# Attention and MLP on one core: a new hand-written order for the first two tiles and three batches

## The chip, the cores and the metric

One NeuronCore of a Trainium2 chip runs the program. The metric is the device time of one execution in microseconds (us). Five engines work from queues of their own, in order, and wait for each other through semaphores: TensorE (PE), VectorE (DVE), ScalarE (ACT), GpSimd (POOL) and SyncE (SP), which here only issues transfers.

## The reference

Attention within a window, eight batches, eight heads, 576 positions, 64 values a head:

```
scores = scale * q @ k^T ; scores = where(0 <= i-j < 128, scores + slope_h * -|i-j|, -1e9)
attn = softmax(scores) ; a = attn @ v
x = a.transpose(0, 2, 1, 3).reshape(4608, 512)
h = x @ w_in                       # 512 -> 2048
g = 0.5 * h * (1 + erf(h / sqrt(2)))
out = g @ w_out                    # 2048 -> 512
```

All arrays are fp32.

## The kernel before

The tokens are cut into nine tiles of 512 (`t` = 0 to 8); a batch of 576 positions fills one tile and a little of the next. A matrix product is made of three fp16 products: each operand is split into a high and a low half, the high half written by ACT, the low half by DVE (`low_part`, L219 or L218), and high by high, high by low and low by high are summed in PSUM. Only batch 0's attention and the second product of tile 0 run in fp32.

Per batch and pair of heads (four pairs, names `_0` to `_3`) the steps are: scores on PE (`sc`, L515), bias added on DVE (`s`, L546; batch 0: on PE, L529), row maxima on DVE, exponentials on ACT (`s<-s,nmax`, L639; batch 0: L590), weights split into `e_main` (high on POOL or ACT, low on DVE), transposed by a transfer (`et<-e_main`, L658; batch 0: by PE and copied by ACT, L618, L626), weighing on PE (`av<-et,vbuf`, L700), and leaving into the tile's slice of `x` (`x<-av`, high L720 on ACT, low on DVE). Before a batch begins, `q`, `k` and `v` are split (`qbuf`, `kbuf`, `vbuf`). The words of the weights are joined and split too (`raw`, `zi`, `wi` for `w_in`; `raw`, `zo`, `wo` for `w_out`; L255 to L277).

Per tile there are sixteen blocks of 128 features: twelve matmuls `h` each (L747), four slices of `x` by three products; a gelu (L764 for tile 0, L770 behind it) on ACT, split by POOL and DVE into `g`; and then four output blocks `o` (L790 in fp32, L793), each copied out by `put` (`ob`, ACT for odd, DVE for even blocks, L804 and L806) and sent off. Each function is a Python generator that issues one or a few instructions between its `yield`s.

Two tables of numbers rule the first part. `ORDER` lists the steps of batches 0, 1, 2 and tiles 0, 1 and the loads that belong to them: each word names a generator (`s1`: scores of pair 1 of batch 0, `S1`, `2S1` the same of batches 1 and 2; `l3`: leaving of pair 3; `H4`, `1H4`: features block 4 of tiles 0 and 1; `g`, `o`, `k`: gelu, output block, put; `i`, `j`, `J`: splitting and joining of weights), and the program goes through the words and advances that generator by one `yield`. The words so set the order in each engine's queue, SP's too. `PSUM_BANKS` gives, in the order in which tiles of PSUM are opened, the bank (0 to 7) that each takes. Tiles 2 to 8 come from a regular loop. A `put` takes one of three rooms `ob`, which the 32-bit gelu results share.

Of the kernel before, what the change touches and what calls it, by code (L numbers as in the profile page):

```python
# [1364 lines left out]
```

## Time and profile before

| | us |
|---|---|
| median of three runs | 885.46 (885.32 to 887.59) |
| profiled execution | 886.68 |
| its span in the trace | 884.8 |
| PE busy | 864.7 (98%) |
| DVE busy | 710.0 (80%) |
| ACT busy | 549.5 (62%) |
| POOL busy | 194.6 (22%) |

The span is what the trace covers from the first to the last instruction; 1.88 us of the execution lie outside of it. PE's matmuls overlap, so its busy time is the time in which at least one runs.

### The profile page before, as it was taken

The numbers are of one execution on the slowest core, as the hardware profiler recorded it, in microseconds if no ns is written. First come the engines' busy times: TensorE is split into PE (matmuls) and PEld (weight loads), VectorE is DVE, ScalarE is ACT, GpSimd is POOL, SyncE is SP. The second block draws the span as 40 slices with busy tenths as digits, with TensorE's granted clock in tenths as the row PEclk, the third lists the DMA queues.
The fourth block names the chain that finished last, engine by engine and source line by source line (L and its number), as shares of the span: only waits on it lengthen the run. The fifth ranks groups of instructions, "written<-read, shape, count | busy, mean of one in ns | idle before, by whom it ended". The sixth has DMA issues, their size and how long they took to land.

```text
span 884.8 us, 18584 instructions
## 1 busy us (share of the span) xinstructions
PE 864.7 (98%) x7428; PEld 478.5 (54%) x7428; DVE 710.0 (80%) x1388; ACT 549.5 (62%) x1149; POOL 194.6 (22%) x412
## 2 busy tenths in 40 slices
PE   5899999999999999999999999999999999999998
PEld 3654454544544445445455545454545454588887
DVE  6999999898858886788678884888477889999871
ACT  7999999787635564554464553567355338744760
POOL 1010010121104521353115521534054310000000
PEclk9899999999999999999999999999999999999999
DMA  9757492545380546225622275234222230001001
GB/s 330 249 160 276 168 216 61 157 138 112 88 253 1 97 78 187 70 62 113 185 73 55 57 159 162 54 54 95 62 56 54 74 71 12 1 13 37 1 1 48
DMA packets 174598, 91.63 MB, mean 104 GB/s; under 512 B 133680, under 2 KB 156336, under 8 KB 174384
## 3 DMA queue, kind: packets, MB, share of 16 engines
q1 hardware_dynamic: 174512, 90.45, 38.3%
q8 instruction: 58, 0.95, 0.5%
q14 instruction: 28, 0.23, 0.1%
HBM read 46.53 MB, written 9.44 MB: 63 GB/s over the span
## 4 chain that ended last, share of the span: by engine, by line
PE 78%; DVE 6%; ACT 2%; DMA 2%; issue 2%; POOL 0%; ACTq 0%; DVEq 0%; POOLq 0%
PE h L747 26%; PE o L793 26%; PE o L790 5%; PE av L700 5%; PE u_out L1082 4%; PE sc L515 3%; PE u L995 2%; PE v L995 2%; DVE g L219 2%; PE z_out L1082 1%; PE x_out L1082 1%; PE y_out L1082 1%; PE v_out L1082 1%; DMA et<-e_main 1%; DVE e_main L219 1%
## 5 line engine op out<-in xcount | busy, mean ns | idle before, releaser
L747 PE MATMUL h<-x,wi 128*128 128x512 f16 x1536 | 339.8, 379 | 2.9 <-ACT g L770 2.0
L747 PEld LDWEIGHTS <-wi 128*128 128x128 f16 x1536 | 148.3, 98 | 184.9 <-issue 9.4
L793 PE MATMUL o<-wo,g 128*128 128x512 f16 x864 | 192.3, 379 | 0.0
L793 PEld LDWEIGHTS <-g 128*128 128x128 f16 x1152 | 110.8, 98 | 132.5
L639 ACT ACTIVATE s<-s,nmax 128x192 f32<-128x192 f32 x252 | 110.9, 441 | 42.0 <-DVE nmax L636 41.9
L219 DVE SCALAR_TENSOR_TENSOR e_main<-s,z,e_main 128x192 f16<-128x192 f32 x252 | 117.6, 509 | 13.5 <-POOL e_main L648 10.4
L771 POOL TENSOR_SCALAR g<-g,sg 128x512 f16<-128x512 f32 x96 | 76.3, 802 | 236.6 <-ACT g L770 229.2
L770 ACT ACTIVATE g<-h,gs 128x512 f32<-128x512 f32 x96 | 63.6, 686 | 86.1 <-PE h L747 56.2
L219 DVE SCALAR_TENSOR_TENSOR g<-g,sg,g 128x512 f16<-128x512 f32 x96 | 80.8, 859 | 31.4 <-POOL g L771 31.4
L648 POOL TENSOR_SCALAR e_main<-s,z 128x192 f16<-128x192 f32 x180 | 89.3, 516 | 66.8 <-ACT s L639 37.9
L546 DVE SCALAR_TENSOR_TENSOR s<-sc,cs,bias_h 128x384 f32<-128x384 f32 x112 | 63.9, 608 | 9.7 <-PE sc L515 9.6
L720 ACT ACTIVATE x<-av,cx 128x128 f16<-128x128 f32 (+6 forms) x52 | 24.6, 481 | 67.2 <-PE av L700 62.8
L793 PE MATMUL o<-wo_first,g 128*128 128x512 f16 x288 | 65.8, 379 | 0.0
L515 PE MATMUL sc<-kbuf,qbuf 64*64 64x192 f16 (+3 forms) x1656 | 48.7, 252 | 10.1 <-DMA kbuf<-kp 5.2
L790 PE MATMUL o<-zo,g 128*128 128x512 f32 x128 | 58.4, 596 | 0.0
L636 DVE TENSOR_REDUCE nmax<-s 128x5 f32<-128x960 f32 (+1 forms) x56 | 56.6, 1044 | 1.0 <-POOL s L552 0.8
L552 POOL MEMSET s<- 64x128 f32 (+1 forms) x112 | 19.3, 172 | 144.8 <-DVE s L546 142.7
L219 DVE SCALAR_TENSOR_TENSOR x<-av,cx,x 128x448 f16<-128x448 f32 (+6 forms) x52 | 24.7, 491 | 29.3 <-ACT x L720 29.2
L639 ACT ACTIVATION_READ_ACCUMULATOR s<-s,nmax 128x1 f32 x252 | 47.1, 187 | 0.0
L700 PEld LDWEIGHTS <-vbuf 128*64 128x64 f16 x1680 | 40.3, 111 | 9.6 <-issue 7.6
L700 PE MATMUL av<-et,vbuf 128*64 128x128 f16 (+1 forms) x1680 | 42.9, 210 | 0.1
L1082 PEld LDWEIGHTS <-g 128*128 128x128 f16 x384 | 37.6, 98 | 4.5
(269 smaller groups left out, 1127.2 us busy)
## 6 DMA issues: line engine op xcount, KB each, us to landing
v<-vp SPq DMA_DIRECT2D x32, 320.0 KB, 5.0
out<-ob SPq DMA_DIRECT2D x34, 256.0 KB, 2.2
raw<-w_in SPq DMA_DIRECT2D x8, 1024.0 KB, 10.5
raw<-w_out SPq DMA_DIRECT2D x8, 1024.0 KB, 5.5
q<-qp SPq DMA_DIRECT2D x7, 1152.0 KB, 6.1
k<-kp SPq DMA_DIRECT2D x7, 1152.0 KB, 7.5
qbuf<-qp SPq DMA_DIRECT2D x4, 288.0 KB, 5.1
kbuf<-kp SPq DMA_DIRECT2D x4, 288.0 KB, 6.7
```

The lines of the kernel that those rows point to most:

```text
L219: return nc.vector.scalar_tensor_tensor(out=dst, in0=src, scalar=scale, in1=high, op0=ALU.mult, op1=ALU.subtract)
L515: done = nc.tensor.matmul(ps[bank][o, n, gap:W], a, m[:, gap:W], start=(i == 0 and (n == 0 or b > 0)), stop=(i == len(terms) - 1 and b > 0 ...
L546: yield nc.vector.scalar_tensor_tensor(out=s[:, bank[0] : bank[0] + k, :], in0=ps[bank][:, 0:k, 0:W], scalar=cs, in1=bias.broadcast_to([P, ...
L639: yield nc.scalar.activation(s[:, i, :], s[:, i, :], AF.Exp, bias=nmax[:, i : i + 1], accum_out=z[:, i : i + 1])
L648: yield nc.gpsimd.tensor_scalar(e[:, i, 0, c], s[:, i], z[:, i : i + 1], 1.0, op0=ALU.mult, op1=ALU.mult)
L700: done = nc.tensor.matmul(av[r, (j - blocks[0]) * QB : (j - blocks[0] + len(js)) * QB], v32s[b][:, hp, kb, r] if b < EXACT else vbuf[:, vi ...
L747: done = nc.tensor.matmul(ph, wi[n][:, a, cc, k * P : (k + 1) * P], x[:, cc, b, :], start=(i == 0), stop=(i == 3 * NCC - 1),)
L770: yield nc.scalar.activation(g32, ph, AF.Gelu, scale=gsc[t, n])
L771: yield nc.gpsimd.tensor_scalar(g[:, r, 0], g32, gsg[t, n], 1.0, op0=ALU.mult, op1=ALU.mult)
L790: done = nc.tensor.matmul(o, g[:, r, c], zo[n][:, n % 2, k * DM : (k + 1) * DM], start=(fc == first), stop=(fc == last))
L793: done = nc.tensor.matmul(o, g[:, r, a, c], wo[n][:, b, k, :], start=(fc == first and i == 0), stop=(fc == last and i == 2),)
L1082: nc.tensor.matmul(ps[name][:, tb], f(d, a)[:, k, tb * P : (tb + 1) * P], w(d, b, k), start=first, stop=True, skip_group_check=True,)
```

## The change

New numbers in `ORDER` and `PSUM_BANKS`. The buffers of a pair (`s`, `nmax`, `z`, `et`) are made when a step first asks for them, no longer by the step of the first part, so that steps may come in another order; for the same reason the join of words looks its target up later and the gelu its `g`. The regular loop is not touched. Two lines of the table, and the code:

```
-z0 z0 z0 b b z1 b z1 z1 z2 b F z2 F s0 m00 m00 s0 m00 x00 x00 x00 x00 s0 x00 n00 n00 s1 m01 z2 x01 x01 m01 z2 x01
+z0 z0 z0 b b s0 s0 s0 m00 m00 m00 z1 z1 z1 x00 x00 m01 x00 x00 x00 z2 m01 x01 b b s1 x01 z2 m10 x01 n00 z2 x10 m10 s1
...
-        raw = raws.pop(n)
+        raw = raws[n]
         lo, hi = raw[:, :, 0], raw[:, :, 1]
-        zi = z.bitcast(I32)
...
+        zi = z().bitcast(I32)
...
-        yield from join_words(n, zi[n])
+        yield from join_words(n, lambda: zi[n])
...
+        def __getattr__(self, name):
+
+            u, hp = self.u, self.hp
+            if name in ("nmax", "z"):
+                made = small([P, NG], f"{name}{u}", 2, tag=name)
+            elif name == "s":
+                made = room([P, NG, W], F32, "s", f"s{u}", 2)
+            elif name == "et":
+                k = 1 if self.b < EXACT else 2
+                made = pool.tile([P, NG * 2 * k, P], F16 if k > 1 else F32, tag=f"et{hp % 2}", name=f"et{u}", bufs=1)
+            else:
+                raise AttributeError(name)
+            setattr(self, name, made)
+            return made
...
-        g = g_of[t, q]
         if t == 0:
-            yield nc.scalar.activation(g[:, r], ph, AF.Gelu, scale=gsc[t, n])
+            yield nc.scalar.activation(g_of[t, q][:, r], ph, AF.Gelu, scale=gsc[t, n])
```

The code lost a few lines above these places, so line numbers differ by one (helpers) to fourteen between the two kernels.

DVE at the leaving of batch 0's pairs, before. `x_410` is `x` of tile 0, `av_3_0` the weighing of pair 3 of batch 0; `zi` and `wi` are words and halves of `w_in`:

```order
L256 TENSOR_SCALAR zi_585,stw_586<-zi_585 128x1024 x2
L266 SCALAR_TENSOR_TENSOR zi_585<-zi_585,raw_363 128x1024
L269 SCALAR_TENSOR_TENSOR zi_585<-raw_363,zi_585 128x1024
L219 SCALAR_TENSOR_TENSOR x_410<-av_2_0_545,scv_450,x_410 128x512
L266 SCALAR_TENSOR_TENSOR zi_585<-zi_585,raw_439 128x1024
L219 SCALAR_TENSOR_TENSOR wi_647<-zi_261,sww,wi_647 128x1024
L185 TENSOR_SCALAR stw_586<-stw_586 128x2
L266 SCALAR_TENSOR_TENSOR zi_261<-zi_261,raw_316 128x1024
L312 TENSOR_TENSOR stw_586<-stw_586 128x1
L219 SCALAR_TENSOR_TENSOR x_410<-av_3_0_650,scv_450,x_410 128x512
```

And after, the same place:

```order
L218 SCALAR_TENSOR_TENSOR x_466<-av_1_0_508,scv_476,x_466 128x512
L255 TENSOR_SCALAR zi_653,stw_654<-zi_653 128x1024
L218 SCALAR_TENSOR_TENSOR x_466<-av_2_0_570,scv_476,x_466 128x512
L255 TENSOR_SCALAR zi_653,stw_654<-zi_653 128x1024
L218 SCALAR_TENSOR_TENSOR x_466<-av_3_0_631,scv_476,x_466 128x512
L218 SCALAR_TENSOR_TENSOR wi_688<-zi_345,sww,wi_688 128x1024
L184 TENSOR_SCALAR stw_654<-stw_654 128x2
L311 TENSOR_TENSOR stw_654<-stw_654 128x1
```

The joins of two words of `zi`, a third join (two of them half done) and one low half of `wi` stood before the slice of pair 3 and stand behind it now.

ACT at the same place, before (`et_3` is the copy of pair 3's transposed weights):

```order
L720 ACTIVATE x_410<-av_2_0_545,scv_450 128x512
L626 COPY et_3_595<-tp_3_5_617 128x512
L626 COPY et_3_595<-tp_3_7_630 128x512
L263 ACTIVATE raw_439<-raw_439 128x1024
L716 COPY tail<-av_3_1_636 128x64
L277 ACTIVATE wi_647<-zi_261,sww 128x1024
L263 ACTIVATE raw_316<-raw_316 128x1024
L720 ACTIVATE x_410<-av_3_0_650,scv_450 128x512
```

And after:

```order
L631 COPY et_3_568<-tp_3_7_615 128x512
L720 ACTIVATE x_466<-av_1_0_508,scv_476 128x512
L254 ACTIVATE zi_653<-raw_478 128x1024
L720 ACTIVATE x_466<-av_2_0_570,scv_476 128x512
L254 ACTIVATE zi_653<-raw_490 128x1024
L720 ACTIVATE x_466<-av_3_0_631,scv_476 128x512
L276 ACTIVATE wi_688<-zi_345,sww 128x1024
L261 ACTIVATE raw_436<-raw_436 128x1024
L261 ACTIVATE raw_490<-raw_490 128x1024
```

The joins and the split have gone behind the slice of pair 3.

ACT at the end of tile 1, before (`ob_1`, `ob_3` are copies of output blocks 1 and 3 of tile 1, `g_2_0` the first gelu of tile 2):

```order
L720 ACTIVATE x_2902<-av_3_3_3078,cx_3_2893 128x192
L422 ACTIVATE vbuf<-v_3_2122,scv_2384 128x2560
L720 ACTIVATE x_1721<-av_3_2_3103,cx_2_2328 128x384
L804 ACTIVATE ob_1_3157<-o_1_2621,so_2719 128x512
L804 ACTIVATE ob_3_3176<-o_3_2576,so_2719 128x512
L770 ACT_TABLE_LOAD
L770 ACTIVATE g_2_0_3208<-h_0_3194,gs_0_3188 128x512
```

And after:

```order
L720 ACTIVATE x_1719<-av_3_2_3086,cx_2_2977 128x384
L804 ACTIVATE ob_1_3128<-o_1_2543,so_1394 128x512
L421 ACTIVATE vbuf<-v_3_2287,scv_2472 128x2560
L720 ACTIVATE x_2921<-av_3_3_3131,cx_3_2914 128x192
L720 ACTIVATE x_2921<-av_1_3_2753,cx_3_2914 128x192
L769 ACT_TABLE_LOAD
L769 ACTIVATE g_2_0_3208<-h_0_3194,gs_0_3188 128x512
```

`ob_3` has moved ten rows forward and `ob_1` stands ahead of the split of `v`; the last copy of the tile is now one of DVE's.

## Rows read from the trace of the kernel before

**Rows 1.** The page: busy time of the engines over the span, with share and instructions.

```profile
PE 864.7 (98%) x7428; PEld 478.5 (54%) x7428; DVE 710.0 (80%) x1388; ACT 549.5 (62%) x1149; POOL 194.6 (22%) x412
```

**Rows 2.** Busy time in five stretches of the span: start and end, length, then busy us (and instructions) of each engine, the granted clock of PE, the busy share of the DMA engines and GB/s.

```profile
0.00:53.00 53.00, 40.95 (x435) 28.36 (x436) 43.42 (x90) 47.82 (x123) 6.05 (x19) 0.94 0.73 242
53.00:165.00 112.00, 111.63 (x791) 53.36 (x791) 105.98 (x217) 105.17 (x188) 6.90 (x21) 1.00 0.67 194
165.00:255.00 90.00, 88.06 (x814) 44.37 (x810) 79.04 (x158) 66.08 (x150) 15.06 (x32) 1.00 0.51 132
255.00:323.00 68.00, 65.98 (x614) 32.58 (x611) 52.64 (x113) 32.68 (x81) 27.67 (x55) 1.00 0.33 79
323.00:884.00 561.00, 558.12 (x4793) 319.85 (x4788) 428.94 (x814) 297.76 (x609) 138.88 (x285) 1.00 0.29 71
```

**Rows 3.** What PE waited for over the whole span: engine, line and output that waited, what released it; us in total, times, longest.

```profile
PE sc L515 <- ACT s L590: 2.7, 4, 1.7
PE tp L618 <- ACT s L590: 2.1, 3, 1.2
...
PE h L747 <- ACT g L770: 2.0, 2, 1.3
```

**Rows 4.** The same columns as rows 2, for 20 to 56 us in steps of 6; the last row is the sum.

```profile
20.00:26.00 6.00, 4.47 (x47) 3.01 (x48) 6.00 (x13) 6.00 (x23) 0.00 (x0) 0.70 1.11 329
26.00:32.00 6.00, 5.90 (x62) 4.63 (x63) 5.96 (x19) 5.49 (x15) 0.35 (x1) 0.73 1.03 375
...
sum 36.00, PE 32.36 PEld 22.68 DVE 35.12 ACT 35.49 POOL 3.48; mean PE 5.39 PEld 3.78 DVE 5.85 ACT 5.92 POOL 0.58
```

**Rows 5.** Timeline of PE, start us, us, engine, line, operation, tiles, count, and idle time before it with what ended it.

```profile
52.58 9.67 PE L747 MATMUL h<-x,wi 128*128 128x512 f16 x44
```

**Rows 6.** Timeline of ACT and of DVE around the fourth slice of `x` of tile 0.

```profile
51.40 1.44 ACT L277 ACTIVATE wi<-zi,sww 128x1024 f16<-128x1024 f32 x1
52.45 1.43 ACT L263 ACTIVATE raw<-raw 128x1024 int32<-128x1024 uint32 x1
53.49 0.95 ACT L720 ACTIVATE x<-av,scv 128x512 f16<-128x512 f32 x1
...
54.14 1.22 DVE L266 SCALAR_TENSOR_TENSOR zi<-zi,raw 128x1024 int32<-128x1024 int32 x1
55.35 0.74 DVE L219 SCALAR_TENSOR_TENSOR x<-av,scv,x 128x512 f16<-128x512 f32 x1
```

**Rows 7.** The same columns as rows 2, from the start to two points: the end of the fourth slice of `x` on DVE, and the end of the last low half of the fourth pair of batch 1.

```profile
0.00:56.09 56.09, 44.04 (x450) 29.77 (x451) 46.52 (x96) 50.91 (x126) 6.05 (x19) 0.94 0.73 240
0.00:158.88 158.88, 146.46 (x1157) 78.50 (x1158) 145.48 (x299) 146.87 (x306) 12.95 (x40) 0.98 0.68 208
```

**Rows 8.** Timeline of PE at the start of tile 2.

```profile
255.11 10.52 PE L747 MATMUL h<-x,wi 128*128 128x512 f16 x48
266.33 2.75 PE L747 MATMUL h<-x,wi 128*128 128x512 f16 x12 [0.69 <-ACT g L770]
...
291.03 1.24 PE L747 MATMUL h<-x,wi 128*128 128x512 f16 x5 [1.30 <-ACT g L770]
```

**Rows 9.** Timeline of ACT there.

```profile
249.75 2.43 ACT L422 ACTIVATE vbuf<-v,scv 128x2560 f16<-128x2560 f32 x1
...
262.02 0.69 ACT L804 ACTIVATE ob<-o,so 128x512 f32<-128x512 f32 x1 [8.79 <-DMA out<-ob]
264.30 1.28 ACT L770 ACT_TABLE_LOAD   x1 [1.59 <-DMA out<-ob]
265.59 1.84 ACT L770 ACTIVATE g<-h,gs 128x512 f32<-128x512 f32 x3
...
273.02 0.69 ACT L770 ACTIVATE g<-h,gs 128x512 f32<-128x512 f32 x1 [2.87 <-PE h L747]
273.73 1.28 ACT L639 ACT_TABLE_LOAD   x1
```

**Rows 10.** Timeline of DVE there.

```profile
267.10 4.46 DVE L219 SCALAR_TENSOR_TENSOR g<-g,sg,g 128x512 f16<-128x512 f32 x4 [4.14 <-POOL g L771]
...
289.17 1.03 DVE L219 SCALAR_TENSOR_TENSOR g<-g,sg,g 128x512 f16<-128x512 f32 x1
```

**Rows 11.** Timeline of PE, the three waits of scores in tile 1.

```profile
172.68 0.83 PE L515 MATMUL sc<-kbuf,qbuf 64*64 64x192 f16 x29 [0.61 <-ACT g L770]
...
208.07 0.88 PE L515 MATMUL sc<-kbuf,qbuf 64*64 64x192 f16 x30 [0.85 <-ACT g L770]
...
222.39 0.69 PE L515 MATMUL sc<-kbuf,qbuf 64*64 64x192 f16 x24 [0.38 <-DVE s L546]
```

**Rows 12.** Timeline of DVE and of PE at the fourth pair of batch 1, and the time from issue to landing of the transposing transfers `et<-e_main` of 120 to 170 us.

```profile
150.89 0.42 DVE L219 SCALAR_TENSOR_TENSOR e_main<-s,z,e_main 128x192 f16<-128x192 f32 x1 [0.21 <-ACT e_main L646]
...
158.47 0.41 DVE L219 SCALAR_TENSOR_TENSOR e_main<-s,z,e_main 128x192 f16<-128x192 f32 x1
...
163.91 1.60 PE L700 MATMUL av<-et,vbuf 128*64 128x128 f16 x66
...
DMA to landing us min/median/max: 3.8/4.2/5.0
```

**Rows 13.** Timeline of DVE and of PE at the first scores of batch 1.

```profile
90.09 2.61 DVE L219 SCALAR_TENSOR_TENSOR kbuf<-k,scq,kbuf 128x2304 f16<-128x2304 f32 x1
...
93.54 1.44 PE L515 MATMUL sc<-kbuf,qbuf 64*64 64x192 f16 x48
```

More of the change, by code (lines that the diff above doesn't have):

```diff
@@ new lines @@
+e0 e0 t0 t1 e1 x30 x30 z W0 t2 s3 j1 e0 n21 a2 x30 L0 m30 x30 z s3 x30 j1 z j0 m31 n30 j1 p0 n30 t0 t1 n30 p0 p0 z t2
+F a3 t1 t1 e0 w0 v0 e1 t3 n21 v0 F p0 e2 e1 e1 W1 F L1 e2 t2 a3 e2 p0 n21 x31 x31 m31 x31 v0 v0 x31 w1 t3 i1 t2 t2 e2
+cl n31 n31 n31 v0 e2 l0 p1 t3 i1 p1 p1 i0 W2 t3 p1 e3 w2 l0 H3 F i0 d d d H2 p1 p0 d L2 e3 j2 j2 e3 e3 H1 t3 H0 j2 W3
+e3 w3 l1 l1 F H1 a4 H2 a4 l2 l2 a5 f a5 H3 lv lv lv H1 H0 H0 p2 l3 l3 H0 i2 i2 j3 H2 H4 lv p2 p2 p1 p2 H3 H4 j5 H2 j5
+p2 a6 j5 j4 H4 H3 H4 f p2 p2 j4 j4 H5 H5 g0 H5 H1 H5 i5 i5 g3 j3 j3 i4 i4 g4 J0 a7 a6 g5 j7 a7 H10 H11 H11 i3 i3 j7
@@ L333, in join_out @@
     def join_out(m):
-        yield from join_words(NWP + m, zo[m][:, m % 2])
+        yield from join_words(NWP + m, lambda: zo[m][:, m % 2])
     most, pwm, k2 = (pool.tile([P, 1], F32, name=n) for n in ("most", "pwm", "k2"))
@@ L532, in scores @@
         yield done
-    def room_for_weights(st):
-        if not hasattr(st, "s"):
-            st.s = room([P, NG, W], F32, "s", f"s{st.u}", 2)
-        return st.s
     def biased(st, banks):
-        b, hp, s, ps, cs = st.b, st.hp, room_for_weights(st), st.ps, csq[st.b]
+        b, hp, s, ps, cs = st.b, st.hp, st.s, st.ps, csq[st.b]
         for bank in banks:
@@ L572, in first_maxima @@
     def first_maxima(st, part):
-        if part == 0:
-            st.nmax = small([P, NG], f"nmax{st.u}", 2, tag="nmax")
         for bank in RANGES[part][2]:
@@ L584, in first_exponentials @@
         r, c, banks = RANGES[part]
-        if part == 0:
-            st.z = small([P, NG], f"z{st.u}", 2, tag="z")
-        s = room_for_weights(st)
+        s = st.s
         for bank in banks:
@@ L621, in turned @@
     def turned(st):
-        st.et = et = pool.tile([P, NG * 2, P], F32, tag=f"et{st.hp % 2}", name=f"et{st.u}", bufs=1)
+        et = st.et
         for bank in BANKS:
@@ L630, in softmax @@
         u, s, e = st.u, st.s, e_main
-        if part == 0:
-            st.nmax = small([P, NG], f"nmax{u}", 2, tag="nmax")
-            st.z = small([P, NG], f"z{u}", 2, tag="z")
         nmax, z = st.nmax, st.z
@@ L653, in low_weights @@
         e = e_main
-        if part == 0:
-            st.et = pool.tile([P, NG * 4, P], F16, tag=f"et{st.hp % 2}", name=f"et{st.u}", bufs=1)
         for i in range(r.start, r.stop):
```

71 lines of the change are left out of this document (33 added, 38 removed).

## The prediction

> **What bounds the kernel now.** I read the page's busy table first, then a table of stretches, then the waits, and only then single stretches of the timeline. TensorE (PE) is busy 98% of the span [rows 1], so only its idle time can be won. The stretches [rows 2] say where that lies: in the first 53.00 us PE is busy for 40.95, so 12.05 are idle; from 53 to 165 it loses 0.37, from 165 to 255 1.94, from 255 to 323 2.02, and in the 561 us behind that 2.88. The steps from tile 2 on (the regular loop, first `h` at 255.11) come in the same order in both kernels, so a change in the time must be a change of when PE gets to about 323 us. The waits [rows 3] name ScalarE (ACT) for nearly all of the loss, and VectorE (DVE) for a little.
>
> In the first 56 us ACT and DVE are the full engines, not PE: from 20 to 56 they idle 0.51 and 0.88 us of 36 [rows 4]. PE becomes dense at 52.58 [rows 5], because the last of the four slices of `x` of tile 0 (`x<-av_3_0`: high half on ACT, low half on DVE) gets there late: ACT does it at 53.49 to 54.44, DVE at 55.35 to 56.09 [rows 6].
>
> **Term A, the start: 2.5 us won.** The order of before and after shows what stands ahead of that slice. On ACT four operations of 128x1024 go behind it (three word joins L263, one split L277), each about 1.05 us from start to start [rows 6]: 4.2 us. ACT had idled only 56.09 - 50.91 = 5.18 up to then [rows 7], and most of that is the first loads, so its half would end near 54.44 - 4.2 = 50.2. On DVE five operations of 128x1024 at 1.2 us go behind (6.0 us), more than it can use: it then waits for ACT. The low halves of slices two to four stand nearly together in after, 0.74 each, so I put the whole slice at 51.8 rather than at the bound 50.2 + 0.74 = 51.0. That is 56.09 - 51.8 = 4.3 earlier.
>
> PE cannot use all of it. When PE becomes dense in before (52.58) it has done all of batch 0 and 21 `h` matmuls, and up to 56.09 it does 16 more at 10.52/48 = 0.219 us [rows 8]. In after the first nine `h0` matmuls that need slice four come behind batch 0 and 24 `h` matmuls. The last three of the nine want 51.8, so the first starts at 51.8 - 6 x 0.219 = 50.5; I take 50.7. In before PE has 24 done at 52.58 + 3 x 0.219 = 53.2. Won: 53.2 - 50.7 = **2.5**. Bounds: 0, if DVE's supply later takes it back, and the 4.3 of the slice itself.
>
> **Term B, the start of tile 2: 2.0 us won.** At 255 to 292 PE waits 0.69 before `h2_4` and 1.30 before `h2_12`, each for a gelu [rows 8]. The gelus are late: ACT's last output copy waits 8.79 us for an output transfer that frees its buffer, and the table load behind it 1.59 for another; the first gelu of tile 2 starts at 265.59 [rows 9], though PE had its input done at 255.11 + 2.6 = 257.7. In after the two ACT copies of tile 1 stand apart (`o1_3` amid the weights of the last pair, `o1_1` ahead of the split of v), the copy that reuses a buffer is DVE's, and ACT's own last copy has a free one. Then come 2.43 of v, two slices of `x` and the load at 1.28 [rows 9], so the gelu can follow `h2_0` by a microsecond or two instead of eight, and the 0.69 goes. The 1.30 is an echo: DVE reaches scores of batch 3 only behind four late low parts (267.10 to 271.56 [rows 10]), the exponentials follow, and nine low weights keep `g` of `h2_8` back to 289.17. With the four gelus done before the scores I expect 1.2 to 2 us less. Both gone: 0.69 + 1.30 = **2.0**; bounds 0 and 2.0.
>
> **Term C, the waits in tile 1: 1.5 us won.** Three short waits, 0.61, 0.85 and 0.38 [rows 11], hit scores of batch 2, two for a gelu that frees a PSUM bank. In after each pair's scores of batch 2 stand in one piece instead of up to three, other banks are named for them, and ACT has four table loads fewer in this part (eight instead of the twelve between the first gelu and tile 2): 4 x 1.28 = 5.1 us of ACT [rows 9], beside PE, on the path only where a gelu is awaited. The two for a gelu should go, 0.61 + 0.85 = **1.5**; the one for DVE stays, since DVE has as much to do as before. Bounds: 0, if the new banks bring like waits, and all three, 1.8. The Trainium skill (ScalarE: Activation LUTs, What ACT_TABLE_LOAD costs) prices a switch at 2.66 us, a drain of about 1.38 beside the load; then the four would free 10.6 us, an estimate, and C would be more certain but no larger. The trace disagrees: the load at 273.73 follows a gelu that ends at 273.71, and the gelu behind the load of 264.30 starts at 265.59, 1.29 after it [rows 9].
>
> **Term D, a new wait in batch 1: 1.5 us lost.** In after PE comes to the weighing of batch 1's fourth pair with 140.9 us of work done (dense spacings summed in its order), in before with 139.6; there it starts at 163.91 and waits for nothing [rows 12]. With A won that is 140.9 + 19.5 = 160.4, 19.5 being what PE has lost by 50.7 (31.2 us of work done). The weights must be there. DVE has 142.5 us of work up to the last low half of that pair, in before 145.48; its idle time in before was 56.09 - 46.52 = 9.6 at slice four and 158.88 - 145.48 = 13.4 at this low half [rows 7], 3.8 more. In after slice four has 40.4 of DVE's work up to its end, so 51.8 - 40.4 = 11.4 idle there and 15.2 here: 142.5 + 15.2 = 157.7. The transposing transfer lands 4.2 later (3.8 to 5.0 [rows 12]): 161.9. PE waits 161.9 - 160.4 = **1.5**; bounds 0, if the small waits shrink, and 4.2, a landing wholly exposed. In before it was 158.88 + 4.2 = 163.1 against 163.91, hidden by 0.8. `k` of batch 1 is as tight: DVE ends it at 92.70 and PE starts at 93.54 in before [rows 13]; in after 85.3 + 12.1 = 97.4 against 77.8 + 19.5 = 97.3, so 0.1, left out.
>
> Other edits cost nothing: the buffers made at first use, the lambda and the `raws` table run while the program is built. The engines' operations are the same in number but for the table loads.
>
> **Sum.** 2.5 + 2.0 + 1.5 - 1.5 = 4.5. The profiled execution took 886.68 (span 884.8 and 1.88 around it), 1.22 above the median of the runs, 885.46; its terms are taken off the median: 885.46 - 4.5 = **881.0**.
>
> **Rivals.** (1) *The start is taken back.* DVE idles only 6.0 of the 112 us behind 53 [rows 2], so an earlier PE may just wait for weights and for `k`: A falls to 0 while C is replaced by like waits. Only B stays: 885.46 - 2.0 = 883.5, which by the 0.3% (2.66 us) that a measurement here tells from no change is the same time. For it: the margins of D. Against: ACT and DVE have the same work less 5.1 us, and it starts no later. (2) *Larger gain.* Slice four passes on all 4.3 and D is hidden: 4.3 + 2.0 + 1.8 = 8.1, so 877.4. (3) *Slower.* All pairs of batch 1 share one `e_main`, so a pair's halves are written only when the transfers of the pair before have read it. If PE weighs the last two pairs as soon as they come, write and landing of each are exposed in turn: the 1.5, two landings of 4.2 and ten low halves at 0.4 make 13.9 against 6.0 won, 893.4. It decides from 6.0 + 2.7 = 8.7 us of waits on. For it: DVE already waits for high halves there, 0.21 us once [rows 12]. Against: PE waits 0.37 in this whole stretch of before [rows 2], and has tile 1's first features to do between the pairs. (4) *The clock.* From 20 to 32 us the granted clock was 0.70 and 0.73, behind waits of PE of up to 1.7 us, and 1.00 from 53 on [rows 2 to 4]. If the new order had such a 12 us stretch in the dense part, at 0.7 it would cost 12 x 0.3 = 3.6: 881.0 + 3.6 = 884.6. The Trainium skill (TensorE: Matmul & The Clock Gate, HAM oscillation) says that idle gaps of PE throttle it again; by that rule a gap moved behind 53 us costs more than itself. The trace agrees as far as it goes: 1.00 in all stretches from 53 us on [rows 2].
>
> **Chances.** Forecast 0.50 (its own range 879 to 882.7, gains of 6.5 to 2.8), taken back 0.19, larger 0.16, slower 0.12, clock 0.03. Faster by over 0.3%: 0.50 + 0.16, and 0.02 of the first rival, 0.68; within: 0.17 + 0.03 = 0.20; slower: 0.12. The range leaves out the slower case and the far end of the larger one: 877.5 to 886.5.
>
> **What would show it.** A: `x<-av_3_0` complete near 52 and PE idle in the first 53 us down by 2 to 3. B: the first gelu of tile 2 within 3 us of its input, no wait of `h` for a gelu at tile 2. C: fewer than 1.9 us idle in tile 1. D: PE waiting one to three us for a transposing transfer near 160. The forecast is wrong if PE's lost time at the middle of batch 1 is not below that of before, or if new waits of scores for gelus replace those of C.

## The result, and the profile after

| | before | changed |
|---|---|---|
| median of the runs, us | 885.46 (885.25 to 887.59, 5 runs) | 890.89 (889.57 to 892.11, 5 runs) |
| ratio, with its 95% interval | 1 | 1.0052 (1.0036 to 1.0069) |
| profiled execution, us (its span) | 886.68 (884.8) | 891.0 (888.9) |

By the ratio, which is one of means, the changed kernel is 0.52% slower; the medians lie 5.4 us apart. One execution of a kernel below, the one with other banks, took 2314.33 us and is left out of its ratio. The forecast was 881.0, faster, with a range of 877.5 to 886.5: wrong in sign, and the time lies outside the range.

The page of the changed kernel, beside [rows 1]: TensorE (PE) has the same work; ScalarE (ACT) has four instructions less, all of them table loads, and 4.6 us less of busy time.

```profile
PE 865.4 (97%) x7428; PEld 479.2 (54%) x7428; DVE 709.0 (80%) x1388; ACT 544.9 (61%) x1145; POOL 198.2 (22%) x412
```

The stretches of the changed kernel, with the columns of [rows 2]:

```profile
0.00:53.00 53.00, 41.23 (x440) 28.67 (x441) 40.93 (x87) 46.61 (x122) 4.27 (x18) 0.97 0.85 275
53.00:165.00 112.00, 110.46 (x753) 52.59 (x752) 108.06 (x221) 102.01 (x185) 6.95 (x22) 1.00 0.59 177
165.00:255.00 90.00, 87.62 (x842) 44.96 (x839) 77.90 (x156) 65.00 (x149) 21.21 (x32) 1.00 0.47 122
255.00:323.00 68.00, 63.83 (x549) 30.97 (x547) 49.07 (x104) 33.22 (x82) 25.01 (x51) 0.97 0.35 87
323.00:884.00 561.00, 560.85 (x4851) 321.01 (x4846) 431.23 (x820) 298.02 (x610) 140.73 (x290) 1.00 0.29 71
```

PE is busy for 0.28 us more than before in the first 53 us, loses 1.54 us from 53 to 165 (before 0.37), 2.38 from 165 to 255 (1.94) and 4.17 from 255 to 323 (2.02), there at a granted clock of 0.97. Behind 323 both kernels do the same work in the same order. (The last row can't be set beside that of before: it ends 4.9 us ahead of the changed kernel's span, and so leaves out the end of its work.)

PE's waits in the changed kernel that [rows 3] have not, or have otherwise (what waited, what released it; us in total, times, longest):

```profile
PE h L747 <- DVE x L218: 3.6, 1, 3.6
...
PE sc L529 <- ACT g L769: 1.8, 2, 1.0
PE av L700 <- DMA et<-e_main: 1.2, 2, 0.9
...
PE h L747 <- ACT g L769: 0.6, 1, 0.6
```

One wait of 3.60 us for VectorE (DVE), of an `h` for `x`, stands in no part of the forecast. It is tile 2's first matmul, `h2_0`. PE around it, as in [rows 8]:

```profile
252.81 2.76 PE L793 MATMUL o<-wo,g 128*128 128x512 f16 x12
259.17 14.81 PE L747 MATMUL h<-x,wi 128*128 128x512 f16 x60 [3.60 <-DVE x L218]
...
295.20 5.12 PE L747 MATMUL h<-x,wi 128*128 128x512 f16 x23 [0.56 <-ACT g L769]
```

The granted clock around it (columns of [rows 2]):

```profile
255.00:260.00 5.00, 1.40 (x7) 0.48 (x6) 4.10 (x4) 1.50 (x3) 0.00 (x0) 1.00 0.90 332
260.00:264.00 4.00, 4.00 (x12) 1.51 (x11) 0.67 (x4) 0.31 (x1) 0.00 (x0) 0.58 0.81 235
264.00:270.00 6.00, 6.00 (x30) 2.71 (x28) 1.50 (x2) 3.04 (x4) 1.76 (x3) 1.00 0.46 150
```

PE stood idle for 3.60 us, and then the granted clock fell: 0.58 of full speed over 260 to 264, that is near the lower of its two levels (1.2 of 2.4 GHz), and back at 1.00 from 264 on. The 60 matmuls of 128x512, those of `h2_0` to `h2_4`, took 14.81 us; without the fall, in the kernels below, the same 60 take 13.11. So the gap cost 3.60 and 1.70 more behind it.

What DVE did meanwhile ([rows 10] begin later):

```profile
250.67 2.61 DVE L218 SCALAR_TENSOR_TENSOR kbuf<-k,scq,kbuf 128x2304 f16<-128x2304 f32 x1
253.20 1.66 DVE L218 SCALAR_TENSOR_TENSOR x<-av,cx,x 128x384 f16<-128x384 f32 x3
255.90 2.88 DVE L218 SCALAR_TENSOR_TENSOR vbuf<-v,scv,vbuf 128x2560 f16<-128x2560 f32 x1 [1.04 <-ACT vbuf L421]
258.70 0.41 DVE L218 SCALAR_TENSOR_TENSOR x<-av,cx,x 128x192 f16<-128x192 f32 x1
```

The last of `x` of tile 2, the three pieces of 384 columns at 253.20, is done at 254.86, and PE had its turn at 255.57. But PE waits until DVE's next `x`, 258.70 to 259.11, which belongs to tile 3. That one does not write what `h2_0` reads. It reads the PSUM bank that `h2_0` will write: in the built program the four buffers of the regular loop's `h` take the banks at addresses 0, 3, 2, 1 in turn, and in the changed kernel address 0 was last held by the weighing of batch 2's fourth pair into tile 3, whose place is the last digit of the new `PSUM_BANKS`. In the kernel before that address was last held by a weighing of the third pair into tile 2, read at 248.29:

```profile
248.29 0.61 DVE L219 SCALAR_TENSOR_TENSOR x<-av,cx,x 128x384 f16<-128x384 f32 x1
```

In the changed kernel, between the slices of `x` that `h2_0` needs and the reading it waits for, stands the low half of v, 2.88 us, itself waiting 1.04 for ACT.

**Where the time went.** "Time lost" at an instruction is its start minus PE's work ahead of it, with the work taken by dense spacings, as in the prediction's term D. Both kernels have the same work ahead of the last place.

| time lost by PE, us, at | before | changed | lost or won between |
|---|---|---|---|
| first scores of batch 1 | 22.6 | 21.1 | start: 1.6 won |
| weighing of batch 1's fourth pair | 24.3 | 23.9 | batch 1: 1.2 lost |
| first weighing of batch 2 behind the last wait of scores | 26.6 | 27.1 | tile 1: 0.9 lost |
| `h2_13` of tile 2 | 28.9 | 33.1 | tile 2: 3.7 lost |

From unrounded values: -1.57 + 1.21 + 0.88 + 3.65 = 4.17 us lost, against 4.1 between the two spans. The 5.4 between the medians is more, because the profiled execution of before lies 1.2 above its own median; the start alone differs by up to 2 us between executions, as shown further down.

### The profile page after: what moved, and what is told of

It is laid out like the page before. It is cut to its first block, busy times and chain, and to the rows that moved or that the text cites. A ratio compares the mean times of both kernels' runs of the same rounds, so it can differ in the third digit from the quotient of the medians.

```text
span 888.9 us, 18597 instructions
## 1 busy us (share of the span) xinstructions
PE 865.4 (97%) x7428; PEld 479.2 (54%) x7428; DVE 709.0 (80%) x1388; ACT 544.9 (61%) x1145; POOL 198.2 (22%) x412
## 4 chain that ended last, share of the span: by engine, by line
PE 72%; DVE 7%; issue 5%; ACT 2%; DMA 1%; POOL 1%; SPq 0%; POOLq 0%; ACTq 0%; DVEq 0%
PE o L793 27%; PE h L747 27%; PE av L700 4%; PE u_out L1082 4%; PE sc L529 3%; PE u L995 2%; PE v L995 2%; DVE e_main L218 1%; POOL g L771 1%; PE z_out L1082 1%; PE v_out L1082 1%; PE y_out L1082 1%; PE x_out L1082 1%; DVE s L555 1%; DMA v<-vp 1%
## 5 line engine op out<-in xcount | busy, mean ns | idle before, releaser
L771 POOL TENSOR_SCALAR g<-g,sg 128x512 f16<-128x512 f32 x96 | 81.8, 858 | 225.9 <-ACT g L769 199.4
L720 ACT ACTIVATE x<-av,cx 128x448 f16<-128x448 f32 (+6 forms) x52 | 24.5, 482 | 61.0 <-PE av L700 59.3
L218 DVE SCALAR_TENSOR_TENSOR x<-av,cx,x 128x448 f16<-128x448 f32 (+6 forms) x52 | 24.8, 492 | 30.1 <-ACT x L720 29.9
```

Of the source, the lines that this page charges most:

```text
L218: return nc.vector.scalar_tensor_tensor(out=dst, in0=src, scalar=scale, in1=high, op0=ALU.mult, op1=ALU.subtract)
L771: yield nc.gpsimd.tensor_scalar(g[:, r, 0], g32, gsg[t, n], 1.0, op0=ALU.mult, op1=ALU.mult)
```

## The experiments

The theory: the loss is the bank, 3.60 us of waiting and 1.70 us of clock. Its rivals: the data of `x` are late and any bank would wait; the clock falls without the gap; the changed code and not the tables costs the time.

**Another bank, nothing else.** The eight banks are opened once at the start in another order, so that the tables keep their names and the addresses behind the names change.

```diff
+    for n in "74520136":
+        psums[-1].tile([P, TT], F32, tag=f"bank{n}", name=f"first{n}", bufs=1)
     banks_of = iter(PSUM_BANKS)
```

> The changed kernel with one thing else: the eight banks are opened once at the start in another order, so that the four banks that the first four feature blocks of tile 2 take belong to tiles read early (o1_1, av2_0 of tile 2, av2_2 and av2_3 of tile 2), and the last weighing of batch 2 (av2_3 of tile 3) lies in a bank of the other group. Theory, bank: the 3.6 us that the first matmul of tile 2 waits at 259.17 are a wait for the bank in which av2_3 of tile 3 lies until DVE has read it at 258.70 to 259.11, behind the split of v. Then the wait goes, and so do the 1.7 us that the first twelve matmuls lose at the lower clock behind it: 890.9 - 5.3 = 885.6. Rival, data: x of tile 2 itself or DVE's queue is late; then nothing changes, 890.9. Rival, wait alone: 3.6 go and the slow matmuls stay, 887.3.

Measured: 886.76 median, ratio to before 1.0009 (0.9999 to 1.002). PE in this kernel at tile 2:

```profile
254.39 13.11 PE L749 MATMUL h<-x,wi 128*128 128x512 f16 x60
...
290.82 7.03 PE L749 MATMUL h<-x,wi 128*128 128x512 f16 x24 [2.63 <-ACT g L771]
```

ACT in this kernel there:

```profile
260.27 1.28 ACT L771 ACT_TABLE_LOAD   x1 [4.80 <-DMA out<-ob]
261.57 0.69 ACT L771 ACTIVATE g<-h,gs 128x512 f32<-128x512 f32 x1
266.48 1.84 ACT L771 ACTIVATE g<-h,gs 128x512 f32<-128x512 f32 x3 [4.22 <-DMA out<-ob]
```

Its stretch from 280 to 300 (columns of [rows 2]):

```profile
280.00:300.00 20.00, 17.37 (x181) 8.60 (x179) 17.41 (x48) 9.26 (x20) 11.07 (x20) 0.91 0.35 61
```

The wait at `h2_0` is gone, and the 60 matmuls take 13.11. So the bank was the cause, not the data. But the time is 1.2 above the 885.6 of the bank theory: a new wait of 2.63 stands at `h2_12`, with a clock of 0.91 in its stretch; the 24 matmuls behind it take 7.03 where 5.34 is usual (below). ACT shows what is late. Its load waits 4.80 us for an output transfer and its second gelu 4.22 for another, so that the second to the fourth come at 266.48, where the first three of before came at 265.59 [rows 9].

**PE kept busy over the gap.** Sixteen matmuls of 128x512 that nobody reads, into a bank that is free, between the last output product of tile 1 and `h2_0`.

```diff
-4q 4q 2x2 2X2 2x3 2x2 2x3 1k1 1k1 2Y3 2X3 2X3 1o2 1k2 1k2 2X1 2X1 1k0 3V 2X2
+4q 4q 2x2 2X2 2x3 2x2 2x3 1k1 1k1 2Y3 2X3 2X3 1o2 zz 1k2 1k2 2X1 2X1 1k0 3V 2X2
...
+    def keep_busy():
+        spare_bank = psums[-1].tile([P, TT], F32, tag="bank7", name="unused", bufs=1)
+        for n in range(16):
+            done = nc.tensor.matmul(
+                spare_bank.rearrange("p (c f) -> p c f", c=2), wi[0][:, 0, 0, 0:P], wi[0][:, 0, 0:2, :],
+                start=(n == 0), stop=(n == 15),
+            )
+        yield done
...
```

> The changed kernel with 16 idle matmuls of 128x512 into a bank that nobody reads (no part of the computation), put between the last output block of tile 1 and the first features of tile 2, where PE waits 3.6 us; 16 x 0.216 = 3.5 us fit into the wait. Theory, clock: behind the wait the first twelve matmuls take 4.3 us instead of 2.6 because the granted clock has fallen while PE idled; with PE kept busy they take 2.6, and the time is 890.9 - 1.7 = 889.2. Rival: the twelve are slow for another reason (weights, banks): 890.9, and a granted clock below 1.00 in 260 to 280 stays.

Measured: 887.73, ratio 1.0029 (1.0018 to 1.004), 3.2 under the changed kernel. PE in this kernel at `h2_0`:

```profile
257.81 13.12 PE L747 MATMUL h<-x,wi 128*128 128x512 f16 x60 [0.15 <-DVE x L218]
```

`h2_0` still starts only when DVE is done (a wait of 0.15 is left), but the 60 matmuls take 13.12 instead of 14.81: 1.69 of the 3.2 is the clock. The other 1.5 agree with the start, which in this execution had lost 19.6 at the first scores of batch 1, not 21.1. So the clock falls because of the gap.

**The code alone.** The changed code with the order and the banks of before:

```diff
-z0 z0 z0 b b s0 s0 s0 m00 m00 m00 z1 z1 z1 x00 x00 m01 x00 x00 x00 z2 m01 x01 b b s1 x01 z2 m10 x01 n00 z2 x10 m10 s1
+z0 z0 z0 b b z1 b z1 z1 z2 b F z2 F s0 m00 m00 s0 m00 x00 x00 x00 x00 s0 x00 n00 n00 s1 m01 z2 x01 x01 m01 z2 x01
...
```

> The changed code (buffers made at first use, targets looked up later) with both tables of before. Every theory: the tables alone move the time, so 885.5 and the same order. If the code had a part, anything else, most likely through buffers that come in another sequence.

Measured: 886.01, ratio 1.0 (0.9991 to 1.0008). Buffers made at first use move nothing that shows, as forecast.

**The bank in the kernel before.** The same eight openings in the order "67051423", so that `h2_0` takes the bank that DVE reads last there.

> The kernel before, with one thing changed: the eight PSUM banks are opened once in another order at the start, so that the bank that tile 2's first h group will take holds the last pair's weighing of batch 2, which VectorE reads out last (in the profile of before that read ends near 256.9, and the first h group starts at 255.11). The bank theory, alone: TensorE waits near 257.0 instead of starting at 255.1, 1.8 us lost, 885.5 + 1.8 = 887.3; if the granted clock falls behind this gap as it did in the changed kernel, 1.7 us more, 889.0. The rival, that the wait in the changed kernel hung on the data of x and not on the bank: nothing moves, 885.5.

Measured: 886.47, ratio 1.001 (1.0002 to 1.0019). PE in this kernel at tile 2:

```profile
256.05 13.11 PE L749 MATMUL h<-x,wi 128*128 128x512 f16 x60 [1.81 <-DVE x L221]
...
290.39 5.34 PE L749 MATMUL h<-x,wi 128*128 128x512 f16 x24 [0.59 <-ACT g L772]
```

The wait appears as expected, 1.81 us, and the clock does not fall behind it (13.11). The median rises by 0.8 only, since the waits for gelus behind it shrink from 0.69 + 1.30 to 0.59 as PE comes later. The mechanism holds in either kernel; what a bank costs depends on how late its reader is, and on what PE would have waited for anyway.

**The two halves apart.** First the new order up to batch 1's first scores (step `S0`), then the rest of before's order; banks renamed where the two didn't fit. The seam:

```diff
-J4 O O O A4 g15 S0 B0 B0 B0 S0 S0 g10 f O f J5 A6 B0 O B0 B0 M00 M00 M00 M00 B0 B0 B0 M01 M00 S1 S1 S1 B1 B1 lQ J4 J4
+J4 O O O A4 g15 g10 f f S0 S1 B0 A6 B1 B1 B1 S0 S0 A5 B1 S1 B0 B0 B0 B0 M00 M00 M00 B1 B0 M00 lQ M00 B0 B0 o J6 M00 B0
...
```

> The changed kernel's order up to the first scores of batch 1 and from there the order of before, less the steps already done (25 of the 144 banks named anew, where the old one was still held). Theory: the start is worth what PE's lost time at 53 us shows, 22.0 in before against 21.0 in the changed kernel, 1.0 us, and the rest of the change costs the difference: 885.5 - 1.0 = 884.5. Rival, taken back: batch 1 waits for weights and k, so 885.5. Rival, the start is itself part of the loss: above 886.5.

Measured: 890.52, ratio 1.0057 (1.0045 to 1.0069). Its wait of scores for DVE (total, times, longest):

```profile
PE sc L529 <- DVE s L555: 4.4, 5, 2.8
```

Its stretch from 53 to 165:

```profile
53.00:165.00 112.00, 107.39 (x721) 51.00 (x719) 106.37 (x215) 98.09 (x184) 8.08 (x22) 0.98 0.55 166
```

The start is as good as any (19.4 lost at the first scores of batch 1), and 8 us are lost again by 121 us, with DVE busy 106.37 of 112. By what was expected this is the third case, a start that is itself part of the loss. I read it otherwise, as a mismatch of the two pieces: the rest of before's order, with 25 banks renamed, can't follow this start. No run shows which it is, so this one says nothing for the new start and nothing against it.

Then the other way round: before's order up to `S0`, the changed kernel's behind it:

```diff
-f g10 A3 J3 A3 p3 q1 v1 J3 H5 q1 O H13 H12 J3 q1 q1 q1 f H13 u1 f g7 H14 g12 g14 O f H9 g9 H13 O H13 q1 O u1 S0 g5
-S1 A4 B0 A6 B1 O g13 B1 B1 S0 S0 A5 B1 J4 S1 B0 B0 B0 B0 M00 M00 M00 B1 B0 M00 lQ M00 B0 B0 H15 o A4 J6 M00 B0 M01
+J3 H5 q1 O H13 H12 J3 q1 q1 q1 f H13 u1 f g7 H14 g12 g14 O f H9 g9 H13 O H13 q1 O u1 p2 g5 H6 H6 H6 H6 H15 g6 H15 H15
+H15 A4 g13 J4 O A4 g15 S0 B0 B0 B0 S0 S0 O J5 A6 B0 O B0 B0 M00 M00 M00 M00 B0 B0 B0 M01 M00 S1 S1 S1 B1 B1 lQ J4 J4 o
...
```

> The order of before up to the first scores of batch 1, and from there the changed kernel's order and banks. The wait for the bank at tile 2's first h group (3.6 us) and the clock behind it (1.7) should stand in the trace as in the changed kernel. If all of the loss comes from there and the new start gains 1.0 to 2.5 us as the traces of the changed kernel and of the kernel with the opened banks show, this kernel is the slowest yet: 890.9 + 1.0 to 2.5 = 891.9 to 893.4. If the start gains nothing that lasts, 890.9. If the two orders are each tied to their own start, as the kernel with the new start and the old rest suggested, more than 893.5.

Measured: 892.28, ratio 1.0083 (1.007 to 1.0095), the slowest. PE in this kernel at `h2_0`:

```profile
262.34 16.08 PE L747 MATMUL h<-x,wi 128*128 128x512 f16 x60 [3.60 <-DVE x L218]
```

The stretch behind the gap:

```profile
262.00:268.00 6.00, 5.66 (x14) 2.08 (x15) 1.83 (x6) 0.29 (x1) 0.00 (x0) 0.50 0.97 299
```

The same 3.60 us at `h2_0`, with a clock of 0.50 in the 6 us behind it: the 60 matmuls take 16.08, 2.97 over 13.11. The wait depends on nothing ahead of `S0`. The median is 1.4 above that of the changed kernel, the mean 2.2. The execution in the trace, 895.11, is the longest of the five; against the changed kernel's it lost 2.4 more up to the first scores of batch 1 and 1.3 more to the clock behind the gap. So the new start is worth something against the old one, and this run can't say how much.

**The gelus of tile 2.** The kernel before, with its last output writes in another order, so that ACT's last one finds a free buffer:

```diff
-2x3 1o3 1k0 1k0 2X1 1k1 1k1 1o2 2X3 1k2 1k2 1k3 1k3
+2x3 1o3 1k0 1k0 2X1 1k1 1k1 1k3 1k3 1o2 2X3 1k2 1k2
```

> The kernel before, with the order of the last two of tile 1's output writes changed, so that ScalarE is not held for 8.8 us at 262.0 by a write whose buffer is still being sent. If the late first gelus of tile 2 (265.6) are what TensorE waits for at tile 2's fifth and thirteenth h groups (0.7 and 1.3 us), 0.7 to 2.0 us are won: 883.5 to 884.8. If those waits have another cause, 885.5.

Measured: 884.40, ratio 0.9985 (0.9977 to 0.9994): faster than both kernels. ACT in this kernel at tile 2:

```profile
252.03 1.25 ACT L804 ACTIVATE ob<-o,so 128x512 f32<-128x512 f32 x2
262.28 1.28 ACT L770 ACT_TABLE_LOAD   x1 [8.99 <-DMA out<-ob]
263.57 1.85 ACT L770 ACTIVATE g<-h,gs 128x512 f32<-128x512 f32 x3
```

PE there:

```profile
254.59 13.11 PE L747 MATMUL h<-x,wi 128*128 128x512 f16 x60
...
288.94 5.34 PE L747 MATMUL h<-x,wi 128*128 128x512 f16 x24 [0.59 <-ACT g L770]
```

Both copies now stand at 252.03, the first gelu at 263.57, 2.0 us earlier than in [rows 9], and of PE's 0.69 and 1.30 [rows 8] 0.59 is left. Term B was right that a late copy holds up the gelus. But the wait of 8.99 for an output transfer has only moved from the copy to the table load.

**Both repairs in the changed kernel.** The banks opened as "47520136"; `1o1`/`1k1` and `1o2`/`1k2` swapped through the end of the order, so that ACT makes the last write, and the first write's transfer sent at once:

```diff
-4q 4q 2x2 2X2 2x3 2x2 2x3 1k1 1k1 2Y3 2X3 2X3 1o2 1k2 1k2 2X1 2X1 1k0 3V 2X2
+1k0 4q 4q 2x2 2X2 2x3 2x2 2x3 1k2 1k2 2Y3 2X3 2X3 1o1 1k1 1k1 2X1 2X1 3V 2X2
...
+    for n in "47520136":
+        psums[-1].tile([P, TT], F32, tag=f"bank{n}", name=f"first{n}", bufs=1)
```

> The changed kernel with the banks opened in another order as before (no wait for the bank at tile 2's first h group), and with tile 1's last output write made by ScalarE instead of VectorE and the first one sent as soon as it is written, so that all four are sent ahead of the next batch's v loads. In the kernel with the opened banks alone, ScalarE's second gelu of tile 2 came at 266.5, and TensorE lost 2.6 us at the thirteenth h group and 1.7 us to the clock behind it. If these came from the late gelus, they go: 886.8 - 2.6 - 1.7 = 882.5, under the 885.5 of before, which would be the gain of the start. If the gelus are late for another reason, 886.8.

Measured: 885.49 (882.75 to 887.08 over 12 runs), ratio 0.9992 (0.9982 to 1.0002). ACT in this kernel at tile 2:

```profile
256.47 0.69 ACT L806 ACTIVATE ob<-o,so 128x512 f32<-128x512 f32 x1
...
261.93 1.28 ACT L771 ACT_TABLE_LOAD   x1 [4.45 <-DMA out<-ob]
263.22 1.84 ACT L771 ACTIVATE g<-h,gs 128x512 f32<-128x512 f32 x3
```

PE in it, at the first weighing and at tile 2:

```profile
27.66 0.69 PE L702 MATMUL av<-et,v 128*64 128x64 f32 x8 [2.07 <-ACT et L633]
...
290.55 5.34 PE L749 MATMUL h<-x,wi 128*128 128x512 f16 x24 [0.56 <-ACT g L771]
```

The stretches of its start:

```profile
20.00:26.00 6.00, 4.22 (x40) 2.79 (x40) 5.75 (x13) 6.00 (x18) 0.00 (x0) 1.00 1.10 333
26.00:32.00 6.00, 4.34 (x34) 2.49 (x35) 5.33 (x10) 6.00 (x20) 0.37 (x1) 0.59 1.06 389
```

The gelus come at 263.22, PE waits 0.56 at `h2_12` and loses no clock: everything that went wrong from 255 us on is mended, and the median is that of before, not the 882.5 expected. Against the kernel before with its own end mended, 884.40, it is 1.1 behind. This execution's start had a clock of 0.59 from 26 to 32, behind a gap of 2.07 us, and had lost 21.6 by the first scores of batch 1. But the twelve executions fall into two groups: five took 882.75 to 883.96, at a mean granted clock of 0.998 to 1.000, and seven, the one in the trace among them, 885.38 to 887.08, at 0.994 to 0.997. The five lie below every execution of the kernel before measured beside them (29, from 884.97 on), and below the 884.04 that the kernel before reached at best with its writes reordered. So the mended order does reach the time expected in some executions, and where the others lose is known only from the one in the trace.

**The start kept busy.** So that kernel once more, with seven idle matmuls of 128x384 in each of the two gaps of 2.0 us:

```diff
+    def keep_busy(bank):
+        for _ in range(7):
+            nc.tensor.matmul(
+                bank[:, 0 : 2 * W], ident, bias_p[:, 0:2].rearrange("p h k -> p (h k)"), start=True, stop=True,
+            )
...
+        if st.b == 0 and hp == 3 and banks[0][0] == 0:
+            keep_busy(ps[banks[0]].rearrange("p n k -> p (n k)"))
...
+            if (b, hp, part) == (0, 0, 1):
+                keep_busy(av)
```

> The last kernel (changed order, banks opened in another order, tile 1's last output write on ScalarE), with seven matmuls of 128x384 bf16 that nobody needs in each of the two places of the start where TensorE stands idle for 2.0 us in every profile of the new order (ahead of the fourth pair's scores, waiting for the scaling of q until 21.0, and ahead of the first weighing, waiting for ScalarE's copy until 27.7). They write into the bank that the waiting work is about to overwrite. Their bank is free from the first gap's begin, and from 26.4 in the second, so they take about 1.1 us of each gap and delay nothing. If the time of the new order's start hangs on the granted clock behind these gaps (in this kernel's profile it was 0.50 from 27 to 33 us, in another of the same order from 29 to 31, and the time lost to then differed by 2 us, 21.3 against 19.2), the clock stays at 1.00 from 20 to 35, the time lost at 45 us is 19.0 to 19.5, and the median 885.5 - 1.8 to 2.3 = 883.2 to 883.7, with less spread between runs than the 882.8 to 887.1 of the last kernel. If ScalarE bounds the start whatever the clock of TensorE, 885.5 and the same spread.

Measured: 886.00 (884.86 to 887.41), ratio 0.9999 (0.999 to 1.0008). Three stretches of this kernel:

```profile
20.00:26.00 6.00, 4.26 (x41) 2.89 (x42) 5.73 (x11) 6.00 (x19) 0.00 (x0) 1.00 1.10 328
26.00:32.00 6.00, 6.00 (x64) 4.38 (x63) 6.00 (x11) 6.00 (x20) 0.38 (x1) 1.00 1.05 389
215.00:220.00 5.00, 3.28 (x38) 1.59 (x33) 5.00 (x8) 4.97 (x15) 0.95 (x3) 0.74 0.01 2
```

PE in it at the last scores of batch 2:

```profile
214.41 0.89 PE L539 MATMUL sc<-kbuf,qbuf 64*64 64x192 f16 x29 [1.01 <-DVE s L565]
216.47 0.24 PE L539 MATMUL sc<-kbuf,qbuf 64*64 64x192 f16 x1 [1.17 <-ACT g L781]
217.26 1.11 PE L539 MATMUL sc<-kbuf,qbuf 64*64 64x192 f16 x23 [0.55 <-DVE s L565]
```

The first half of the expectation came true: the clock is 1.00 through the start, and PE has lost 19.7 at the first scores of batch 1 instead of 21.6. That the idle matmuls kept the clock up isn't shown by this: with the same start and without them it was 1.00 in both stretches in the kernel kept busy at `h2_0` too. The second half didn't come true: in this execution nothing of the gain reaches the end. In tile 1 PE now comes to the last scores of batch 2 at 213.1, waits 1.01, 1.17 and 0.55 us within 4 us, and the clock falls to 0.74 behind that. By tile 2 it has lost 28.3, no less than the 28.0 of the last kernel. In the two kernels that came there at 214.0 (other banks, kept busy at `h2_0`) the waits were 1.7 and 1.4 us with no fall of the clock, and of the 2.1 us by which the first of them had lost less at the start than the last kernel (19.5 against 21.6), 1.8 were still there at `h2_0` (26.2 against 28.0). A good start can pass this place, then; why it did not here, 0.8 us earlier, one trace can't tell.

## Why the prediction was wrong, point by point

The same places in the traces of eight kernels, one execution each; the code alone and the two halves are left out. Idle matmuls count as lost time.

| time lost by PE, us | first scores of batch 1 | fourth pair of batch 1 | after tile 1's waits | `h2_0` | `h2_13` |
|---|---|---|---|---|---|
| before | 22.6 | 24.3 | 26.6 | 26.9 | 28.9 |
| before, last writes reordered | 21.7 | 23.2 | 26.1 | 26.4 | 26.9 |
| before, bank read last | 21.5 | 23.0 | 25.6 | 27.8 | 28.3 |
| changed | 21.1 | 23.9 | 27.1 | 31.0 | 33.1 |
| changed, other banks | 19.5 | 22.7 | 26.1 | 26.2 | 30.4 |
| changed, kept busy at `h2_0` | 19.6 | 22.7 | 25.7 | 29.6 | 30.1 |
| changed, banks and writes | 21.6 | 24.8 | 27.9 | 28.0 | 28.5 |
| the same, start kept busy | 19.7 | 21.8 | 28.2 | 28.3 | 28.7 |

**The step that failed: "the gelu can follow `h2_0` by a microsecond or two" in term B.** It took `h2_0` itself to stand where it stood, and the sum has no term for its start. I asked whether its input `x` would be there, and it was, at 254.86. I did not ask whose bank it takes over. The diff of `PSUM_BANKS` names the bank in its last digit, and the new order names the reader's place in DVE's queue: behind the low halves of q, of k and of v, which take 2.62, 2.61 and 2.88 us in the kernel before too, with three pieces of `x` between them. None of that was weighed. The wait of 3.60 and the 1.70 of clock make 5.3 us, more than the whole gain forecast (4.5). Of the 2.0 that B was to bring, `h2_4`'s 0.69 went and 1.30 became 0.56, 1.4 less: 5.3 - 1.4 = 3.9, where the table has 3.7. But that 1.4 is not B's doing: PE came 3.60 us later, so it waited less for the same gelus, and with the bank mended 2.63 stand at `h2_12`.

**Why B's own wait persisted.** The ACT copy found a free buffer, as I wrote. But the gelus wait for the output transfers themselves, whose buffers their own outputs take over: 4.80 and 4.22 with the banks mended, 8.99 in the reordered kernel before. I had read the 1.59 ahead of the load [rows 9] as a part of the delay that goes with the other 8.79.

**A, 2.5 won: about 1.6 measured, from single executions that differ by 2.** Slice four of `x` was to be done at 51.8; here are ACT's and DVE's halves:

```profile
50.89 0.71 ACT L720 ACTIVATE x<-av,scv 128x512 f16<-128x512 f32 x1
...
52.42 0.75 DVE L218 SCALAR_TENSOR_TENSOR x<-av,scv,x 128x512 f16<-128x512 f32 x1
```

ACT is done at 51.60 (50.2 was the bound used), but on DVE a 1.21 us maximum of weights goes ahead of the low half, so the slice ends at 53.17. The means over the traces of the table give the same 1.6: 20.3 lost with the new start (five, 19.5 to 21.6) and 21.9 with the old one (three, 21.5 to 22.6). Without the trace whose start was kept busy it is 1.5; the three traces outside of the table (19.4 with the new start, 21.6 and 23.4 with the old one) point the same way. What the start loses differs by 2 us between executions of one order, with the granted clock from 20 to 32 us: 0.72 and 1.00 in the changed kernel's two windows of 6 us, 1.00 and 0.72 with other banks, 1.00 and 1.00 when kept busy at `h2_0`. The clock alone does not rank them: other banks lost 19.5 with a 0.72 in it, kept busy 19.6 without. I had taken the start of one execution as the kernel's.

I also laid nearly all of PE's loss to ACT. The longest of PE's waits in the kernel before, which [rows 3] leave out, is for the first load, 5.2 us of the 12 idle ones of the first stretch:

```profile
PE sc L515 <- DMA kbuf<-kp: 5.2, 1, 5.2
```

**D, 1.5 lost: right, 1.2 measured.** Batch 1 lost 1.2 more than in before (2.85 against 1.64). PE in the changed kernel, at the third and the fourth pair, and then at tile 1's scores, as in [rows 11, 12]:

```profile
156.45 1.60 PE L700 MATMUL av<-et,vbuf 128*64 128x128 f16 x66 [0.34 <-DMA et<-e_main]
...
164.84 1.60 PE L700 MATMUL av<-et,vbuf 128*64 128x128 f16 x66 [0.87 <-DMA et<-e_main]
...
175.84 1.62 PE L529 MATMUL sc<-kbuf,qbuf 64*64 64x192 f16 x53 [0.86 <-ACT g L769]
...
217.02 0.24 PE L529 MATMUL sc<-kbuf,qbuf 64*64 64x192 f16 x1 [0.97 <-ACT g L769]
217.80 0.68 PE L529 MATMUL sc<-kbuf,qbuf 64*64 64x192 f16 x23 [0.54 <-DVE s L555]
```

The fourth pair waits 0.87 for its transposing transfer and the third 0.34, 1.2 together; I had put all of it at the fourth.

**C, 1.5 won: wrong sign, 0.9 lost.** In place of 0.61, 0.85 and 0.38 stand 0.86, 0.97 and 0.54. "0, if the new banks bring like waits" was its lower bound; they brought longer ones. The three make 0.5 of the 0.9; the rest is not traced to a wait. I counted it as a gain that each pair's scores stand in one piece. But a piece wants five banks at once: the last pair's second piece of work waits for a gelu's bank at 217.02 and for DVE at 217.80. That this is the cause is read from the waits, and no run takes it apart. That the place can limit what a start brings is read from two traces: coming 3 us earlier than the kernel with banks and writes mended, the one kept busy at its start waits 2.73 there instead of 1.41, with the fall of the clock on top.

**The rivals.** "The start is taken back" (19%) is what happens ahead of tile 2. From the first scores of batch 1 to the end of tile 1's waits the old order loses 4.0 to 4.4, the new one 6.0 to 6.6 (8.5 with the fall of the clock), 2.1 more, against 1.6 won by the start. So in these traces the new order with its end mended is about the old one's equal, as its median is; the five executions of 882.75 to 883.96 did better, and none of them has a trace. The rival took another way than I wrote: D, which the sum had, and C with the wrong sign. "The clock" (3%) came true in its mechanism, a gap of PE moved into the dense part, at a place where I hadn't looked for it: 1.70 us, not 3.6. The Trainium skill (TensorE: Matmul & The Clock Gate, HAM oscillation) says that idle gaps of PE throttle it again, so that a gap costs more than itself. The trace agrees, 0.58 over 260 to 264 behind 3.60 us idle, and I should have carried the rule into every term that moves a wait, not into one rival of its own. "Slower" was given 12% for a mechanism, the single `e_main`, that did not act: PE's waits for these transfers are 1.2 us in all.

**What stays open.** Why the clock of the start differs between executions of the same program; what the five short executions of the mended kernel did otherwise; how much the new start is worth in the median; and whether tile 1's second loss hangs on the one-piece scores or on the bank names.

## What to carry to other kernels

A new bank or buffer table moves waits to the first user of each place: for each first matmul of a stage, list the last reader of the bank it takes and that reader's place in its queue, even where the matmul's own data are early. A gap on TensorE in a dense stretch (3.60 and 2.63 us here, not 1.81) can cost itself and a slower stretch behind it, so the first wait of a stage is worth more than its length. A gain at the start is not yet a gain of the kernel: the waits of the next stages can take it back, so each of them has to be looked at with PE coming earlier. And one execution is not the kernel: the start of one order differed here by 2 us between executions.

## What the runs showed of the hardware

- One gap of TensorE of 3.60 us was followed by a granted clock near the lower level, and cost 1.70 us more in one kernel and 2.97 in another; a gap of 2.63 was followed by 0.91 over 280 to 300, and 24 matmuls behind it took 7.03 us instead of 5.34; a gap of 1.81 was followed by no fall. Three short ones of 1.01, 1.17 and 0.55 us close together were followed by 0.74. The length of a wait is thus not all that it costs.
- Matmuls whose result nobody reads, put into the gap at tile 2, kept the clock up (13.12 us for the 60 matmuls behind it instead of 14.81) and won 1.7 us. At the start, where the clock was 1.00 in an execution without them too, the median shows no gain by them (886.00 against 885.49).
